# Dense products as pairs of 64-row halves with two outputs in two banks, in cycles of two attention steps

## The chip, the cores and the metric

The kernel runs on one core of a Trainium2 chip. The metric is device microseconds of one execution. Before the change the median of three runs is 1954.51 us (1954.01 to 1956.67).

## The reference

A layer norm of x (2048 x 512), and on it an attention block (32 heads of 16) and a gated MLP side by side; both are added to x.

```python
def _A_ref(x, wqkv, wo):                       # H = 32, Dh = 16
    qkv = (x @ wqkv).reshape(B, S, 3, H, Dh).transpose(2, 0, 3, 1, 4)
    q, k, v = qkv[0], qkv[1], qkv[2]
    p = softmax(einsum("bhqd,bhkd->bhqk", q, k) * Dh ** -0.5)
    o = einsum("bhqk,bhkd->bhqd", p, v)
    return o.transpose(0, 2, 1, 3).reshape(B, S, D) @ wo
def _B_ref(x, w_in, w_sp, b_sp, w_out):        # F = 1792, Fh = 896
    z = gelu(einsum("bsd,df->bsf", x, w_in))
    z2 = layernorm(z[..., Fh:])
    g = einsum("ts,bsf->btf", w_sp, z2) + b_sp[None, :, None]
    return einsum("bsf,fd->bsd", z[..., :Fh] * g, w_out)
xn = layernorm(x)
return x + _A_ref(xn, wqkv, wo) + _B_ref(xn, w_in, w_sp, b_sp, w_out)
```

## The kernel before, in words

Attention is cut into 1024 **steps**, one for each pair of heads (16), block of 512 queries (4) and block of 128 keys (16). A step has four pieces of work. `scores` (L978, tile `st`) makes the scores of two heads, 128 keys x 512 queries each: two TensorE matmuls that contract 50 rows, one on the upper and one on the lower half of the array. `exp` (L62, tile `pf`) is one ScalarE instruction over both (128 x 1024). `pv` (L952, tile `o`) multiplies the exponentials by V, in groups of four matmuls that each take 32 columns of the array; each such matmul of the program stands as two instructions in the trace (2560 in the program, 5120 in the trace). Ahead of the scores by LEAD = 27 steps runs a pass for the row maxima: `max_mm` (L656, tile `mx`), two matmuls that contract 48 rows, and `max_red` (L664), one VectorE reduction over 128 x 1024. After every 16 maxima five short VectorE instructions (`max_fin`, L677 to L683) and a round trip through DRAM put the maxima into the rows 48 and 49 of the query operand.

Everything else on TensorE is called **dense** here: q and k of the later heads (`qk`), the two halves of the MLP's first product (`z2p`, `z1p`), the spatial product (`sp`), the MLP's output (`mo`) and the attention's output (`ao`). `mm3` (L174 to L176) makes each product of fp32 operands from three matmuls over 128 rows (high x high, low x high, high x low), into one bank of PSUM. A dense tile is evicted by ScalarE or VectorE, and GpSimd does most of the elementwise work behind it.

The order of every engine is written by one loop over `half`. Two halves make a cycle of three steps. The first half issues scores, maximum, scores, the V products of earlier steps and the exponentials, the second half maximum, scores, maximum, and then as many dense products as a `credit` allows. The generators in `queue` yield the price of each dense product; `side` and `bg` hold the elementwise work that is let in a little per half; a clock of `HALF` us per half keeps account of GpSimd. Before step 0, 18 halves do maxima and dense products alone.

PSUM has eight banks: three tiles of two banks turn between scores and maxima (`spsum`), one bank takes dense products (`d`), one the V products (`o`).

Of the kernel before, what the change touches and what calls it, by code (L numbers as in the profile page):

```python
# [16 lines left out]
P = 128  # L17
S = 2048
D = 512
# [14 lines left out]
LEAD = 27  # L34
PF = 6
DENSE = 931
HALF = 2.7
# [3 lines left out]
def fused_block(ctx, tc, x, wqkv, wo, w_in, w_spT, b_sp, w_out, out):  # L41
# [14 lines left out]
    wide = []  # L56
# [43 lines left out]
    left = [0]  # L100

# [9 lines left out]
    now = [-2 * LEAD // 3 - 1]  # L111
# [18 lines left out]
    def later(k, fn, *args):  # L130
        late.append((now[0] + k, fn, args))
# [25 lines left out]
    def dpsum(nm, tag="d", n=1):  # L157
        left[0] = n
# [14 lines left out]
    def mm3(acc, lh, ll, rh, rl, first, last):  # L173
        nc.tensor.matmul(acc, lh, rh, start=first, stop=False)  # L174
        nc.tensor.matmul(acc, ll, rh, start=False, stop=False)  # L175
        nc.tensor.matmul(acc, lh, rl, start=False, stop=last)  # L176

# [26 lines left out]
    def prepare(out, loads, freed=None):  # L204
# [3 lines left out]
        while loads or flight or made:  # L208
# [8 lines left out]
            if loads and len(rawfree) > 0 and clock() >= rawfree[0] and (freed is None or freed and now[0] >= freed[0]):  # L217
# [4 lines left out]
                flight.append((now[0] + 2, k, begin(*a)))  # L222
# [51 lines left out]
    def turn_x(g, lo=0, hi=4):  # L274

        tiles = [spsum(f"xT{g}_{lo}_{c}") for c in range(3)]
        sl = slice(lo * P, hi * P)
        for c in range(ND):
            for i in range(lo, hi):
                nc.tensor.transpose(tiles[c % 3][:, c // 3, i * P:(i + 1) * P], xs[g, i][:, c * P:(c + 1) * P], ident)  # L280
        for c in range(ND):
# [3 lines left out]
            split(t[:, 0, sl], t[:, 1, sl], tiles[c % 3][:, c // 3, sl], (hi - lo) * P)  # L285
# [19 lines left out]
    def qk_group(m, g, w, tags=("d",)):  # L305
        for a in range(2):
            if now[0] < -2 and m:
                tags = ("d", "o")
            acc = dpsum(f"qk{m}_{a}_{g}", tags[a % len(tags)], ND)
            for c in range(ND):  # L310
                t = xnT[g, c]
                mm3(acc, w[a][:, 0, c * P:(c + 1) * P], w[a][:, 1, c * P:(c + 1) * P], t[:, 0, :], t[:, 1, :], c == 0, c == ND - 1)
                yield 650 + 0.5 * (c == ND - 1)
            if m == 0:
                run(qk_split(m, g, a, acc))
                yield 0
                continue
            raw_ = t512(f"qr{m}_{a}_{g}")
            act(raw_, acc, AF.Copy, 512)
            side.append(qk_split(m, g, a, raw_))  # L320
            yield 0
# [17 lines left out]
    def qk_rest():  # L339
        for g in range(NG):  # L340
            for m in range(1, 4):
                if m == 3 and g + 1 < NG:
                    fetch_xnT(g + 1, 1 if now[0] >= 0 else 0)
                while (m, 1) not in wq:
                    yield -1.5
# [4 lines left out]
                yield from qk_group(m, g, [wq[m, a] for a in range(2)])  # L350


    def v_tile(t, ws, mid=None):
        acc = dpsum(f"v{t}", "do"[t % 2])
# [15 lines left out]
    def gelu_out(x, u, n):  # L370

        gps(0.0011 * n).tensor_scalar(u, u, 1.0, 1.0, ALU.mult, ALU.add)
        gps(0.0024 * n).tensor_mul(x, x, u)

    def z2_norm(t, z):
# [7 lines left out]
        act(u, u, AF.Tanh, FH, scale=GC)  # L383
        late_ = t >= NT - 3
        if late_:
            act(u, u, AF.Identity, FH, bias=1.0)
        yield
        if late_:
            gps(0.0024 * FH).tensor_mul(z, z, u)
        else:  # L390
            gelu_out(z, u, FH)
# [18 lines left out]
        act(z, z, AF.Identity, FH, bias=rs[:, 2:3], scale=rs[:, 1:2])  # L410
        for j, (lo, w) in enumerate(((0, 512), (512, 384))):
            yield
# [4 lines left out]
            for a in range(2):  # L417
                store(z2scr[:, lo // P:(lo + w) // P, a, t, :], hl[:, a, :w].rearrange("p (f q) -> p f q", q=P), 1 + a)

    def z2_all():  # L420
        ws = w2
        wide.append(1)
# [8 lines left out]
        yield -3  # L431
        while len(ws) < 2 * ND:
            yield -1.5
        for t in range(NT):
# [3 lines left out]
            if t == NT - 2:  # L438
                wide.clear()
                prime()  # L440
                freed.append(now[0])
                bg.append(prepare(w1, [(f, f"w1_{f}", w_in[:, f * P:(f + 1) * P], D, ND) for f in range(NF)], freed))
            z = piece(f"z2_{t}").bitcast(F32).rearrange("p a b -> p (a b)")
            for j in range(2):
                acc = dpsum(f"z2p{t}_{j}", n=ND)
                for c in range(ND):
                    sl = slice(c * P, (c + 1) * P)
                    mm3(acc[:, :448], xt[:, 0, sl], xt[:, 1, sl], ws[c, j][:, 0, :448], ws[c, j][:, 1, :448], c == 0, c == ND - 1)
# [688 lines left out]
```

## Time and profile before

| what | value |
|---|---|
| median of the runs | 1954.51 us |
| span of the profiled execution | 1953.7 us, so 0.8 us below the median |
| TensorE busy | 1936.4 us (99%), 12559 matmuls |
| VectorE busy | 1373.9 us (70%) |
| ScalarE busy | 1233.1 us (63%) |
| GpSimd busy | 725.8 us (37%) |
| DMA | 284.23 MB, mean 145 GB/s |
| first maximum, first scores, last scores | 83.6, 138.1 and 1940.4 us |

Busy TensorE time is modelled from pipelined matmuls whose recorded durations overlap. The distance between two starts therefore says more than a duration does, and the view of the chain that ended last gives such distances directly.

### The profile page before, as it was taken

What the parts mean: (1) busy time and instruction counts of PE and PEld (TensorE: products, weight loads), DVE (VectorE), ACT (ScalarE), POOL (GpSimd) and SP (SyncE); (2) the same over time, 40 slices, a digit from 0 to 9 for tenths busy, and PEclk for the clock granted to TensorE, in tenths of its full rate; (3) what the DMA queues carried; (4) which work ended last, traced back from release to release, by engine and by line L of the source; (5) the groups of instructions that cost most, each with busy time, mean ns of one, the idle gap of its engine ahead of it and who ended that gap; (6) DMA issues with size and microseconds to landing.
All of it is one profiled execution on the core that took longest, in us unless ns stands there. A gap on an engine that the chain in (4) does not pass through costs nothing.

```text
span 1953.7 us, 32440 instructions
## 1 busy us (share of the span) xinstructions
PE 1936.4 (99%) x12559; PEld 1049.1 (54%) x12559; DVE 1373.9 (70%) x1567; ACT 1233.1 (63%) x1406; POOL 725.8 (37%) x789
## 2 busy tenths in 40 slices
PE   9999999999999999999999999999999999999998
PEld 7765555555555555555555555555555555555443
DVE  5357777777767677777777777777777777777872
ACT  5346778888777665656566656665566655555664
POOL 3334268889776931025122531017112400002100
PEclk9999999999999999999999999999999999999999
DMA  7566343463545635364545845346354735355323
GB/s 276 197 221 179 103 114 101 130 178 104 148 133 152 185 115 142 97 177 153 140 138 161 204 130 127 110 123 205 105 160 138 202 111 135 119 147 166 105 74 114
DMA packets 228466, 284.23 MB, mean 145 GB/s; under 512 B 34440, under 2 KB 133400, under 8 KB 225432
## 3 DMA queue, kind: packets, MB, share of 16 engines
q1 hardware_dynamic: 216360, 272.38, 48.3%
q0 software_dynamic: 2592, 8.46, 1.1%
q10 hardware_dynamic: 9360, 1.31, 0.4%
q8 instruction: 99, 1.62, 0.3%
q14 instruction: 55, 0.45, 0.1%
HBM read 188.51 MB, written 93.58 MB: 144 GB/s over the span
## 4 chain that ended last, share of the span: by engine, by line
PE 93%; DVE 2%; POOL 2%; DMA 1%; ACT 1%; issue 1%; SPq 0%; DVEq 0%; POOLq 0%; ACTq 0%
PE o L952 23%; PE mx L656 15%; PE st L978 15%; PE sp L174 7%; PE sp L176 5%; PE sp L175 5%; PE qk L174 2%; PE mo L174 2%; PE z1p L174 2%; PE qk L175 1%; PE qk L176 1%; PE z2p L174 1%; PE mo L175 1%; PE mo L176 1%; PE z1p L176 1%; PE z1p L175 1%
## 5 line engine op out<-in xcount | busy, mean ns | idle before, releaser
L664 DVE TENSOR_REDUCE mm<-mx 128x2 f32<-128x1024 f32 x1024 | 1222.1, 1222 | 498.6 <-PE mx L656 494.1
L62 ACT ACTIVATE pf<-st 128x1024 f32<-128x1024 f32 x1024 | 1028.6, 1025 | 621.7 <-PE st L978 589.1
L952 PE MATMUL o<-pf,vall 128*32 128x512 f32 (+1 forms) x5120 | 510.8, 513 | 0.0
L656 PE MATMUL mx<-kst,qst 48*128 48x512 f32 x2048 | 447.4, 434 | 2.5 <-ACT pf L62 1.6
L978 PE MATMUL st<-qst,kst 50*128 50x512 f32 x2048 | 443.2, 431 | 1.1 <-DVE mm L664 0.9
L656 PEld LDWEIGHTS mx<-kst,qst 48*128 48x128 f32 x2048 | 192.3, 185 | 268.3 <-ACT pf L62 175.6
L978 PEld LDWEIGHTS st<-qst,kst 50*128 50x128 f32 x2048 | 192.5, 185 | 159.6 <-issue 85.4
L952 PEld LDWEIGHTS o<-pf,vall 128*32 128x32 f32 x5120 | 131.5, 109 | 233.3 <-issue 211.1
L174 PE MATMUL sp<-wsp,zs 128*128 128x512 f32 x448 | 194.1, 433 | 0.3 <-DVE z1i L572 0.2
L579 POOL TENSOR_TENSOR z1i<-z1i,hhl 128x512 f32<-128x512 f32 x28 | 36.1, 1289 | 425.6 <-DVE z1i L572 395.1
L176 PE MATMUL sp<-wsp,zs 128*128 128x512 f32 x448 | 175.9, 393 | 0.0
L175 PE MATMUL sp<-wsp,zs 128*128 128x512 f32 x448 | 175.8, 392 | 0.0
L174 PEld LDWEIGHTS sp<-wsp,zs 128*128 128x128 f32 x448 | 83.8, 187 | 68.8 <-issue 51.7
L176 PEld LDWEIGHTS sp<-wsp,zs 128*128 128x128 f32 x448 | 84.1, 188 | 19.7
L175 PEld LDWEIGHTS sp<-wsp,zs 128*128 128x128 f32 x448 | 84.4, 188 | 12.1
L200 POOL CAST wo<-wo0r 128x512 fp32r<-128x512 f32 x1 | 0.6, 612 | 190.0 <-DMA wo0r<-in_wo 190.0
L329 POOL TENSOR_TENSOR qkhl<-qr,qkhl 128x512 fp32r<-128x512 f32 x24 | 31.0, 1290 | 75.0 <-ACT qkhl L62 75.0
L174 PE MATMUL z2p<-w,xt 128*128 128x448 f32 x128 | 51.3, 400 | 0.0
L174 PE MATMUL mo<-wout,hp 128*128 128x512 f32 x112 | 48.5, 433 | 0.6 <-DVE xr L616 0.4
L176 PE MATMUL z2p<-w,xt 128*128 128x448 f32 x128 | 46.9, 366 | 0.0
L175 PE MATMUL z2p<-w,xt 128*128 128x448 f32 x128 | 46.7, 365 | 0.0
L715 POOL TENSOR_TENSOR ob<-ob 128x512 f32<-128x512 f32 (+1 forms) x16 | 20.6, 1288 | 65.8 <-DMA ob<-rscr 59.1
(384 smaller groups left out, 1985.4 us busy)
## 6 DMA issues: line engine op xcount, KB each, us to landing
zs<-z2scr SPq DMA_DIRECT2D x112, 512.0 KB
escr<-e SPq DMA_DIRECT2D x60, 256.0 KB
hscr<-hhl SPq DMA_DIRECT2D x28, 512.0 KB
xscr<-xnT POOLq DMA_DIRECT2D x16, 512.0 KB, 4.8
qscr<-qkhl SPq DMA_DIRECT2D x16, 512.0 KB
kscr<-qkhl SPq DMA_DIRECT2D x16, 512.0 KB
xt<-xscr SPq DMA_DIRECT2D x64, 128.0 KB
z2scr<-z2hl SPq DMA_DIRECT2D x32, 256.0 KB
```

The lines of the kernel that those rows point to most:

```text
L62: return nc.scalar.activation(out, in_, func, **kw)
L174: nc.tensor.matmul(acc, lh, rh, start=first, stop=False)
L175: nc.tensor.matmul(acc, ll, rh, start=False, stop=False)
L176: nc.tensor.matmul(acc, lh, rl, start=False, stop=last)
L200: gps(0.6).tensor_copy(t[:, 0, :n], rw[:, :n])
L329: gps(1.3).tensor_sub(hl[:, 1 - a, :], src, hl[:, a, :].bitcast(F32))
L579: gps(1.3).tensor_add(z1, z1, hl[:, 1, :].bitcast(F32))
L656: nc.tensor.matmul(acc[:, j, :], qst[p % 2][rows, tt * P:(tt + 1) * P], kst[p % 2][rows, kc * 512:(kc + 1) * 512], start=True, stop=True)
L664: dve(1024).tensor_reduce(mmax[i // 16][:, :, t, kc], mstep.pop(i), AX.X, ALU.max)
L715: gps(1.3).tensor_mul(both[rows, 0, :], both[rows, 0, :], both[rows, 2, :])
L952: nc.tensor.matmul(acc[cols:cols + VW, a:a + w], vpack(kt - 1 + r, 2 * p + j), pf[:, j * 512 + a:j * 512 + a + w], start=(kt == 1 and a == ...
L978: nc.tensor.matmul(st[:, j, :], kst[p % 2][rows, kt * P:(kt + 1) * P], qst[p % 2][rows, c * 512:(c + 1) * 512], start=True, stop=True)
```

## The change

1. A dense product over 128 rows is cut into its upper and lower 64 rows (`lane`). Two outputs are made side by side in two banks (`d0`, `d1`): for two passes, `halves` runs output 0 on one half of the array and output 1 on the other, and then the other way round. An output without a partner (`whole`, the seventh column block of `z1p` and `sp`) has its halves in the two banks, and they are added at the eviction. One of the two outputs is evicted by VectorE, one by ScalarE.
2. A cycle is two steps, one per half. The first half issues a maximum, scores and all dense products, the second a maximum, scores and one round of V products (four matmuls of 512 columns for two steps).
3. PSUM: one tile of two banks for scores, three single banks for maxima, two for dense products, one for V products. `max_red` becomes two reductions over 128 x 512.
4. LEAD is 28 halves of one maximum each. The delays, the gating of `side` and `bg`, and the prices (now one per pair of matmuls) are restated in the new halves. The bias of the spatial product is added before the product with z1 and not after it. In the last group of `ao` 32 rows of zeros fill up 96 rows to 128. The tanh and the normalisation of `z2p` go in two instructions of half the width.

The core of the diff:

```diff
-LEAD = 27
+LEAD = 28
-HALF = 2.7
+HALF = 1.72
+SWAP, END = 1.25, 1.5
+    def spsum(nm):
+        return ps.tile([P, 2, 512], F32, tag="s", name=nm, bufs=1)
-    def spsum(nm):
+    def msum(nm):
         turns[0] += 1
-        return ps.tile([P, 2, 512], F32, tag=f"s{turns[0] % 3}", name=nm, bufs=1)
+        return ps.tile([P, 512], F32, tag=f"m{turns[0] % 3}", name=nm, bufs=1)
+    def lane(acc, half, prod, start, stop):
+        rows = slice(64 * half, 64 * half + 64)
+        nc.tensor.matmul(acc, prod[0][rows], prod[1][rows], start=start, stop=stop)
+    def halves(accs, parts, done=None):
+        flip = 0
...
+                    for j in range(3):
...
+                        for half in range(2):
+                            u = half ^ flip
+                            lane(accs[u], half, prods[u][j], first, last)
...
+                    yield END if last else SWAP if turn_ else 1
+                if step == 0:
+                    flip ^= 1
+    def evict(u, dst, src, n=512):
+        if u:
+            act(dst, src, AF.Copy, n)
+        else:
+            dve(n).tensor_copy(dst, src)
-        acc = mstep[i] = spsum(f"mx{i}")
+        accs = mstep[i] = [msum(f"mx{i}_{j}") for j in range(2)]
-        dve(1024).tensor_reduce(mmax[i // 16][:, :, t, kc], mstep.pop(i), AX.X, ALU.max)
+        for j, acc in enumerate(mstep.pop(i)):
+            dve(512).tensor_reduce(mmax[i // 16][:, j, t, kc:kc + 1], acc, AX.X, ALU.max)
-        for half in range(-2 * LEAD // 3, 2 * (N // 3 + 4)):
...
+        for half in range(-LEAD, N + 6):
...
+            max_mm(m)
+            if w == 0 and n is not None:
+                scores(n)
+            dense(half)
+            if w == 1 and n is not None:
+                scores(n)
...
+            if w == 1 and 0 <= b - 2 < N:
+                pv(b - 1)
+            if n is not None:
+                exp(n)
+            max_red(m)
```

What the recorded order has now is shown at three places. The first is TensorE in the stage of the spatial product (`sp`), one cycle long, from the last dense product of a cycle to the first of the next. Before, with `o` the V products and `sp` over 128 rows:

```order
L176 MATMUL sp_3_10231<-wsp_2_9062,zs_3_0_9983 128x512
L978 MATMUL st_10241<-qst_86,kst_88 128x512 x2
L656 MATMUL mx_10244<-kst_88,qst_86 128x512 x2
L978 MATMUL st_10247<-qst_86,kst_88 128x512 x2
L952 MATMUL o_1_10044<-pf_10175,vall 32x512 x2
L952 MATMUL o_1_10044<-pf_10199,vall 32x512 x2
L952 MATMUL o_1_10044<-pf_10209,vall 32x512 x2
L952 MATMUL o_1_10044<-pf_10224,vall 32x512 x2
L656 MATMUL mx_10264<-kst_88,qst_86 128x512 x2
L978 MATMUL st_10267<-qst_86,kst_88 128x512 x2
L656 MATMUL mx_10270<-kst_88,qst_86 128x512 x2
L174 MATMUL sp_3_10231<-wsp_3_9080,zs_3_0_9983 128x512
```

TensorE at the same stage of the change, where `sp_2_0` and `sp_2_1` are the two outputs and each row of them is one half of 64 rows:

```order
L189 MATMUL sp_2_1_13178<-wsp_12_12584,zs_3_3_13520 128x512
L189 MATMUL sp_2_0_13177<-wsp_12_12584,zs_2_3_13518 128x512
L799 MATMUL mx_0_13672<-kst_88,qst_86 128x512
L799 MATMUL mx_1_13673<-kst_88,qst_86 128x512
L1112 MATMUL st_13676<-qst_85,kst_87 128x512 x2
L1103 MATMUL o_2_13551<-pf_13627,vall 32x512 x2
L1103 MATMUL o_2_13551<-pf_13643,vall 32x512 x2
L799 MATMUL mx_0_13691<-kst_88,qst_86 128x512
L799 MATMUL mx_1_13692<-kst_88,qst_86 128x512
L1112 MATMUL st_13695<-qst_85,kst_87 128x512 x2
L189 MATMUL sp_2_1_13178<-wsp_12_12584,zs_3_3_13520 128x512
L189 MATMUL sp_2_0_13177<-wsp_12_12584,zs_2_3_13518 128x512
```

Between two groups of dense products there were three scores, three maxima and one visit of V products; now there are two maxima, two scores and one visit of four V matmuls.

The second place is VectorE in the same stage: before, one reduction a step.

```order
L664 TENSOR_REDUCE mm_13916<-mx_14117 128x2
L664 TENSOR_REDUCE mm_13916<-mx_14123 128x2
L664 TENSOR_REDUCE mm_13916<-mx_14147 128x2
L677 TENSOR_REDUCE mrow<-mm_13916 128x2x4
L678 TENSOR_REDUCE mn_14167<-mm_13916 128x8
```

VectorE in the change, around the eviction of one of the two `sp` outputs (`hhl`):

```order
L808 TENSOR_REDUCE mm_17052<-mx_0_17300 128x1
L808 TENSOR_REDUCE mm_17052<-mx_1_17301 128x1
L808 TENSOR_REDUCE mm_17052<-mx_0_17317 128x1
L808 TENSOR_REDUCE mm_17052<-mx_1_17318 128x1
L689 TENSOR_TENSOR hhl_6_17338<-sp_6_1_16986,hhl_6_17338 128x512
L808 TENSOR_REDUCE mm_17052<-mx_0_17349 128x1
```

Each reduction has become two, and the eviction stands between the reductions of two steps.

The third place is ScalarE there. Before, with `e` the eviction of a block of V products:

```order
L62 ACTIVATE pf_8594<-st_8585 128x1024
L62 ACTIVATE pf_8604<-st_8591 128x1024
L62 ACTIVATE e_3_8616<-o_3_8406 128x512
L62 ACTIVATE pf_8618<-st_8610 128x1024
L62 ACTIVATE pf_8640<-st_8631 128x1024
```

ScalarE in the change, with `hhl` the eviction of the other `sp` output:

```order
L63 ACTIVATE pf_17334<-st_17321 128x1024
L63 ACTIVATE hhl_6_17338<-sp_6_0_16985 128x512
L63 ACTIVATE pf_17360<-st_17353 128x1024
L63 ACTIVATE e_0_17364<-o_0_17015 128x512
L63 ACTIVATE pf_17391<-st_17374 128x1024
```

Over the whole of the change's order 321 of the 1023 places between two exponentials hold one other ScalarE instruction, one holds two, and the rest none; before, 163 held one and 54 held two to four.

More of the change, by code (lines that the diff above doesn't have):

```diff
@@ L110, in fused_block @@
     late = []
-    now = [-2 * LEAD // 3 - 1]
+    now = [-LEAD - 1]
     pool = [-1000.0]
@@ new lines, in whole @@
+    def whole(accs, part, done=None):
+        for i in range(len(part)):
+            while True:
+                prods = part[i]()
+                if prods is not None:
+                    break
+                yield -2
+            for j in range(3):
+                last = i == len(part) - 1 and j == 2
+                for half in range(2):
+                    lane(accs[half], half, prods[j], i == 0 and j == 0, last)
+                rem[0] = 3 * (len(part) - i) - j - 1
+                if j < 2:
+                    yield 1
+            if done:
+                done(0, i)
+            yield END if last else 1
@@ L274, in turn_x @@
     def turn_x(g, lo=0, hi=4):
-        tiles = [spsum(f"xT{g}_{lo}_{c}") for c in range(3)]
+        two = spsum(f"xT{g}_{lo}")
+        banks = [two[:, 0, :], two[:, 1, :]] + [msum(f"xT{g}_{lo}_{c}") for c in range(2)]
         sl = slice(lo * P, hi * P)
@@ L505, in z1_all @@
+                if end_ and f > 1:
+                    freed.extend([now[0] + 1] * len(fs))
                 yield 0
```

597 lines of the change are left out of this document (323 added, 274 removed).

## Prediction

> **What bounds the kernel now.** I read the page first, then the chain that ended last in the middle of the spatial product, then the instructions in order of time around one exponential, then the first and last uses of the score tile. From the page:
>
> ```profile
> span 1953.7 us, 32440 instructions
> ...
> PE 1936.4 (99%) x12559; PEld 1049.1 (54%) x12559; DVE 1373.9 (70%) x1567; ACT 1233.1 (63%) x1406; POOL 725.8 (37%) x789
> ...
> PE 93%; DVE 2%; POOL 2%; DMA 1%; ACT 1%; issue 1%; SPq 0%; DVEq 0%; POOLq 0%; ACTq 0%
> ...
> L664 DVE TENSOR_REDUCE mm<-mx 128x2 f32<-128x1024 f32 x1024 | 1222.1, 1222 | 498.6 <-PE mx L656 494.1
> L62 ACT ACTIVATE pf<-st 128x1024 f32<-128x1024 f32 x1024 | 1028.6, 1025 | 621.7 <-PE st L978 589.1
> ```
>
> TensorE carries 93% of the chain, and VectorE and ScalarE wait for TensorE: 494.1 us for maxima, 589.1 us for scores. So the kernel lasts as long as TensorE's own sequence. What a piece of it costs is in the chain, where each row runs until the next begins. One cycle of three steps, and one V visit of the next:
>
> ```profile
> 900.31 0.43 PE sp L174
> 900.74 0.23 PE sp L175
> ...
> 902.35 0.23 PE sp L176
> 902.58 0.43 PE st L978 x2
> 903.01 0.24 PE mx L656 x2
> 903.25 0.24 PE st L978 x2
> 903.49 1.43 PE o L952 x16
> 904.91 0.43 PE mx L656 x2
> 905.34 0.23 PE st L978
> 905.57 0.24 PE mx L656 x2
> 905.82 0.44 PE sp L174
> ...
> 909.02 1.85 PE o L952 x16
> ```
>
> Three prices stand here. A dense product over 128 rows takes 0.23 us, and so does a pair of 48- or 50-row matmuls on the two halves of the array. The first product after a change of shape (128 rows, two halves, four column strips) takes 0.43, so a change costs 0.20. A V visit: by the order both visits are of 16 trace instructions, the first half of 256 and half of 512 columns, the second all of 512; they differ by 0.42, which is one round of four at 512 (and two at 256). The visit that the change leaves, two trace rounds of 512, is therefore 1.43 - 0.42 = 1.01 us, its change of shape included. The cycle is 905.82 - 900.31 = 5.51 us, of which four changes of shape are about 0.7.
>
> For the mean of all cycles, and for both ends of the program:
>
> ```profile
> L656 PE MATMUL mx<-kst,qst x2048: 383/399/626, 83.6 to 1899.0; 48*128 48x512 f32 x187
> L978 PE MATMUL st<-qst,kst x2048: 386/396/794, 138.1 to 1940.4; 50*128 50x512 f32 x187
> ```
>
> From 138.1 to 1940.4 are 1802 us for 1023 steps, **1.76 us a step**, or 3.52 for two. Ahead stand 83.6 us of preparation and 54.5 us in which maxima run alone; behind the last scores are 1953.7 - 1940.4 = 13.3 us.
>
> **The change, part by part.** *Shapes.* If dense halves of 64 rows are of one shape with scores and maxima, both changes around a dense group go: 0.40 us a cycle, 341 times, 136 us. V visits rise from 341 to 512; each costs 1.01 - 2 x 0.42 = 0.17 and the 0.20 of the maximum behind it, so 171 x 0.37 = 63 us come back. The number of products stays: 2880 pairs of halves against 2880 whole ones, 0.23 each, by the rows of `mx` and `st` above. As a sum of TensorE alone, a cycle of two steps with D dense pairs is now: first half, score to score, (2 + D) x 0.23; second half, score 0.23, V visit 1.01, maximum 0.43, 1.67. (0.23 is 902.58 - 900.74 by eight products.)
>
> *One score tile.* This adds a wait that the trace of before does not have: with three tiles of two banks the next scores never waited for the last exponential. Now scores n+1 write where exponential n reads. Its links can be read off:
>
> ```profile
> 904.85 0.50 PE L656 MATMUL mx<-kst,qst 48*128 48x512 f32 x2
> 905.18 0.40 PE L978 MATMUL st<-qst,kst 50*128 50x512 f32 x2
> 905.42 0.40 PE L656 MATMUL mx<-kst,qst 48*128 48x512 f32 x2
> 905.68 1.03 ACT L62 ACTIVATE pf<-st 128x1024 f32<-128x1024 f32 x1 [0.51 <-PE st L978]
> ```
>
> ```profile
> 1940.98 1.02 ACT L62 ACTIVATE pf<-st 128x1024 f32<-128x1024 f32 x1 [2.12 <-PE st L978]
> 1942.05 0.20 PEld L952 LDWEIGHTS o<-pf,vall 128*32 128x32 f32 x6 [0.24 <-ACT pf L62]
> ```
>
> Scores at 905.18, exponential at 905.68: 0.50. The exponential: 1.02. Its end at 1942.00 releases a weight load at 1942.05: 0.05. And a matmul whose weights were not loaded ahead loses what the row at 904.85 loses against the next one, 0.33 against 0.24: 0.10 rounded. Score to score can't be less than 0.50 + 1.02 + 0.05 + 0.10 = **1.68 us** (the unrounded starts give 1.675). Behind the waiting scores stand the dense group, the V round and the next maximum, so this floor is TensorE's in each half. The second half (1.67) sits on it. The first half exceeds it from D = 6 on (8 x 0.23 = 1.84); with D = 5 it is 1.61 and waits. The 448-column products of `z2p` take less:
>
> ```profile
> 302.98 0.20 PE z2p L175
> ```
>
> Six of them and two pairs make 1.66, on the floor again.
>
> Counted over the whole order of the change, the 512 cycles have these D: 37 none, 29 one to four, 92 five, 286 six (61 of them `z2p`), 28 seven, 40 eight. First halves: 37 + 29 + 92 + 61 = 219 at 1.675 are 367 us, 225 at 1.84 are 414, 28 at 2.07 are 58, 40 at 2.30 are 92; second halves: 512 at 1.675 are 858. **Sum 1789 us**, 1.75 a step against 1.76 now. So the saved changes of shape are nearly all given back: 37 cycles without dense products and the floor take about 70 us of them, and the loop has more dense work than before, since fewer products run ahead of it (below).
>
> *Ahead of the loop.* Maxima alone: 28 halves, with 96 dense pairs by the order (216 whole products before, so 120 are moved into the loop, 28 us). TensorE needs (96 + 28) x 0.23 = 29 us. VectorE now reduces twice over 512. A reduction of 512 is not in the trace; the rows next to it are:
>
> ```profile
> 91.14 4.62 DVE L664 TENSOR_REDUCE mm<-mx 128x2 f32<-128x1024 f32 x4 [1.26 <-PE mx L656]
> 1947.89 1.89 DVE L839 TENSOR_TENSOR fin<-al,fin 128x512 f32<-128x512 f32 x3 [1.59 <-PE al L821]
> L776 DVE TENSOR_TENSOR fin<-ao,fin 128x512 f32<-128x512 f32 x16 | 10.9, 680 | 6.3 <-PE ao L176 6.3
> ```
>
> Three 512-wide operations end 1.89 us after the first starts, so one follows another after (1.89 - 0.68) / 2 = 0.60; four 1024-wide reductions follow each other by (4.62 - 1.23) / 3 = 1.13. Bounds for a pair are thus 1.13, if nothing is added, and 1.36, two whole durations of 0.68; I take 2 x 0.60 = 1.20, the closest row. Then 28 x 1.20 = 33.6, four evictions of 0.60 and one group of closing instructions of 0.8 make 37 us: VectorE sets this stage, and the first scores come at 83.6 + 37 = 120.4, 18 us sooner than now (15 to 22 us by the bounds).
>
> *VectorE in the loop.* 2 x 1.20 = 2.4 us in a cycle of 3.35 to 3.53, against 1.13 in 1.76. Three single banks let it lag by one reduction. The closing group fits:
>
> ```profile
> 112.02 0.19 DVE L677 TENSOR_REDUCE mrow<-mm 128x8 fp32r<-128x32 f32 x1
> ...
> 112.63 0.21 DVE L683 STREAM_TRANSPOSE ms<-mrow 128x32 f32<-128x32 f32 x1
> ```
>
> ```profile
> L397 DVE BATCH_NORM_STATS2 zst<-z 128x6 f32<-128x448 f32 x32 | 18.3, 613 | 0.0
> L398 DVE BATCH_NORM_AGGREGATE zmv<-zst 128x2 f32<-128x12 f32 x16 | 3.3, 209 | 0.6
> ```
>
> The closing group takes 0.82 us in 64 cycles, where 0.9 to 1.1 are free. Only the statistics of `z2p` (two at 0.61 and one at 0.21, 1.43) exceed that, by at most 0.5 in 16 cycles; between 0 and 8 us, I take 0.
>
> *ScalarE.* Between the end of an exponential and the next one's start lie 0.05 + 0.10 + 0.50 = 0.65 us. The one other instruction that the order has in 321 of these gaps is of 512 columns or less, 0.60 to 0.63:
>
> ```profile
> 1943.23 0.60 ACT L62 ACTIVATE e<-o 128x512 f32<-128x512 f32 x1 [1.23 <-PE o L952]
> ```
>
> It costs nothing if its input is there in time, and its own lateness if not. I take 0; the other end is a rival below. GpSimd's additions behind evictions and the DMAs keep their number (797 against 793 rows, 1089 on SP in both) and lie beside TensorE; GpSimd is busy for 37% of the span.
>
> *The end.* Four small products `nd` and five visits of `al` lie in the last halves and add about 6 us to the floor; behind the last scores the same 13.3 us follow.
>
> **Sum:** 120.4 + 1789 - 1.7 (the last half lies behind the last scores) + 6 + 13.3 = 1927, and with 4 us for evictions that wait for the last dense pair of their own half (76 groups at 0.05, the release above) 1931. The profiled execution lies 0.8 below the median, so **1932 us**, 1.2% less. Its own range: 1917, if the wait for weights (0.10) is hidden in the second halves and the first ones of D = 5, to 1955, with VectorE at its upper bound in the lead (5), the statistics (8), and 0.01 us on each half of the loop.
>
> **The rivals.** *TensorE's sum decides* (0.11). If exponentials let the score tile go sooner than their end, only products count: 512 x 1.67 + (1024 + 2400) x 0.23 + 384 x 0.20 = 1719, in all 1862. Against it speaks the release row at 1942.05; for it, that TensorE has waited for nothing so far.
>
> *The gaps on ScalarE* (0.19, slower). The other instruction of a gap starts late where it waits for dense products of its own half, for GpSimd or for a buffer, and each microsecond of that is then in the chain through the single score tile, as it was not with three. At 0.15 us on 321 places it costs 48 us: 1980. It decides from 0.08 us on, where the sum passes 1958. For it: the gap of 0.65 leaves 0.02 to 0.05 us. Against: first halves with D of 6 and more have 0.17 us besides, and the order keeps to one instruction in a gap.
>
> *A second matmul is not free* (0.04, slower). The trace shows at most three pairs in a row, and the change has runs of ten. The rows give 0.23 to 0.24 for a pair; if every dense pair takes 0.24, that is 0.01 x 2880 = 29 us: 1961, and a little less already decides. Against it speaks the difference of 0.42 above: 16 trace instructions in two rounds fit into it at 256 columns, 0.21 for eight loads and matmuls, more than a pair asks for. [...]
>
> *The change does not do what it says* (0.03). If 64-row halves count as another shape than 50-row ones, 475 dense groups keep their 0.40 us: 190 us more, 2122. Against: 48 and 50 rows follow each other at 0.23.
>
> **How the numbers follow.** Forecast 0.63: 0.54 of it lies below 1950.6, 0.06 within 0.2% of 1954.5 (what a measurement can tell from no change), 0.03 above. The first rival is faster (0.11), the other three slower (0.26), of the ScalarE rival 0.03 still within 0.2% and 0.03 below. So faster 0.68, same 0.09, slower 0.23. The range from 1885 to 1980 leaves out the first rival's core and the far ends of the slower ones, about 0.2.
>
> **What would show it.** The start of scores n to n+1 alternates between 1.84 and 1.68 us in `sp`; weight loads of `st` wait for ScalarE's `pf` as the longest of all waits; TensorE's dense pairs follow at 0.23 with no 0.43 around them; first scores near 120; VectorE's reductions 0.65 to 0.69 each. The forecast is wrong if dense pairs take more than 0.24, if scores in cycles without dense products come closer than 1.6 or farther than 1.75, or if ScalarE's other instructions end after the next scores are ready.

## The result and the profile after

The changed kernel takes **1972.3 us** (median of 4 runs, 1965.9 to 1975.9) against 1955.6 (4 runs, 1954.0 to 1957.3): ratio 1.0081, 95% interval 1.0062 to 1.0101. It is slower by 16.7 us (0.8%), where 1.2% faster was forecast; the forecast of 1932 is 40 us too low. The page of the changed kernel, in the parts that were shown of before:

```profile
span 1971.1 us, 37250 instructions
...
PE 1920.7 (97%) x14415; PEld 1078.4 (55%) x14415; DVE 1463.7 (74%) x2614; ACT 1268.2 (64%) x1430; POOL 730.6 (37%) x794
...
PE 89%; ACT 4%; DVE 4%; issue 1%; POOL 1%; DMA 1%; DVEq 0%; SPq 0%; ACTq 0%; POOLq 0%
...
L808 DVE TENSOR_REDUCE mm<-mx 128x1 f32<-128x512 f32 x2048 | 1307.2, 684 | 377.7 <-PE mx L799 372.9
L63 ACT ACTIVATE pf<-st 128x1024 f32<-128x1024 f32 x1024 | 1050.3, 1026 | 590.4 <-PE st L1112 574.9
...
L799 PEld LDWEIGHTS mx<-kst,qst 48*128 48x128 f32 x2048 | 218.6, 184 | 486.5 <-DVE mm L808 434.3
...
L1112 PEld LDWEIGHTS st<-qst,kst 50*128 50x128 f32 x2048 | 199.9, 185 | 117.0 <-ACT pf L63 75.6
```

TensorE is still the chain, with 89% of it where it had 93%. ScalarE and VectorE (4% each, 1% and 2% before) have taken the rest. The chain over one ordinary cycle of the changed kernel, in a dense product of the first MLP half:

```profile
661.71 0.43 PE mx L799 x2
662.13 0.26 PE st L1112 x2
662.39 1.39 PE z1p L189 x12
663.78 0.23 PE mx L799 x2
664.02 0.23 PE st L1112 x2
664.25 0.99 PE o L1103 x8
```

Six pairs take 1.39 us, 0.23 each, with no 0.43 at either edge: the halves share the shape of scores and maxima. A V round with its change of shape is 0.99, forecast 1.01. The prices hold in the whole loop too. Measured from the starts of all 1024 pairs of scores, sorted by the number D of dense pairs that the order puts between them:

| half | count | forecast | mean | median |
|---|---|---|---|---|
| first, D = 0 | 37 | 1.675 | 1.62 | 1.59 |
| first, D = 5 | 92 | 1.675 | 1.64 | 1.64 |
| first, D = 6 in `z2p` | 61 | 1.675 | 1.73 | 1.70 |
| first, D = 6 elsewhere | 225 | 1.84 | 1.88 | 1.86 |
| first, D = 7 | 28 | 2.07 | 2.09 | 2.09 |
| first, D = 8 | 40 | 2.30 | 2.44 | 2.31 |
| second | 511 | 1.675 | 1.73 | 1.68 |

The medians are right within 0.09 us. The means of the second halves and of D = 8 are not: a few halves are far longer. Both ends of the loop, from the views of the two tiles:

```profile
L799 PE MATMUL mx<-kst,qst x2048: 386/491/794, 83.4 to 1904.1; 48*128 48x512 f32 x187
```

```profile
L1112 PE MATMUL st<-qst,kst x2048: 386/404/793, 124.1 to 1954.9; 50*128 50x512 f32 x187
```

First scores came at 124.1 (forecast 120.4: +3.7); from there to the last scores are 1830.8 us (1797.3 with the allowances: +33.5); 16.2 follow (13.3: +2.9). These are the 40 us, and 33 of them lie in the loop.

**Where in the loop.** With the measured prices (the median of each row, and 1.62 for D = 0) the order sums to 1790 us, 3 more than the 1787 of the forecast for the same 1023 halves. 41 us stand above the prices, of which the forecast had allowed 10. 30 of the 41 stand in 32 halves. Four places hold 20.9: the first exponentials (124 to 134, 5.5), a single block of `z1p` (682 to 695, 4.4), and two in the spatial product (1028 to 1037, 4.4; 1430 to 1441, 6.6). Four visits of `al`, which the allowance foresaw, hold 3.1. The chain at the largest place of the changed kernel:

```profile
1425.35 5.07 DMA wsp_11r<-in_w_spT
...
1433.13 1.26 POOL wsp L279
1434.39 0.22 POOL os L853
...
1434.63 0.35 DVE os L855
1434.98 0.56 DVE mm L808
...
1435.58 0.79 PE mx L799
1436.37 0.43 PE st L1112 x2
1436.80 3.41 PE sp L189 x16
```

Read it downwards: a block of weights takes 5.07 us to land; GpSimd stands before it in its own order, then splits it and the next; behind them is a small addition of sums (`os`), whose reciprocal VectorE must do before its maxima; TensorE waits for a bank of the maxima. The other place in the spatial product has the same reciprocal in its chain, and the waits of the changed kernel have just these two:

```profile
DVE os L855 <- POOL os L853: 9.0, 2, 4.9
```

The kernel before has no such wait. Its GpSimd stands before blocks of these weights as long (23.2 us in all, 20.8 now), but each of its 16 reciprocals begins 3.4 us or more after the addition has ended. So at these two places the lateness itself came with the new order. The block of `z1p` is the seventh, the one without a partner, whose halves are added at the eviction:

```profile
681.52 0.59 ACT z L63
...
682.20 0.69 DVE z L607
682.89 0.61 DVE mm L808
...
683.54 0.49 PE mx L799
```

The addition waits for ScalarE's copy, and the maxima wait behind it. This alone costs 0.6 us. At the first exponentials an eviction of `qr`, its split and a row of 1.28 us without a tile (ACT_TABLE_LOAD) stand ahead on ScalarE.

At the largest place the rows after the wait are long: eight pairs in 3.41 us, 0.43 each. The windows of the changed kernel show why (the columns are the busy time of each engine; the last three are granted clock, DMA share and GB/s):

```profile
676.00:684.00 8.00, 7.83 (x60) 4.57 (x58) 5.95 (x10) 5.19 (x6) 5.39 (x7) 1.00 0.00 0
686.00:696.00 10.00, 9.96 (x40) 4.43 (x39) 4.91 (x12) 4.69 (x5) 4.77 (x5) 0.51 0.21 79
...
1430.00:1434.00 4.00, 1.77 (x13) 0.38 (x11) 0.00 (x0) 1.02 (x1) 3.30 (x4) 0.97 0.99 320
1434.00:1440.00 6.00, 4.42 (x20) 3.51 (x22) 2.69 (x5) 1.02 (x1) 4.76 (x7) 0.50 0.62 204
```

At each of the four places TensorE's granted clock falls to half (0.50), for 3.4 to 10.2 us, 27 us in all. In the 3.4 us ahead of these stretches 4, 12, 11 and 5 matmuls began, where the median of the loop is 26. These stalls are thus paid twice: once as a wait and once in longer rows (0.43 a pair for 0.23 at 1436.80); in `z1p`, whose next cycles hold no dense products, the second part is nearly all. Of the kernel before, the trace has one such stretch in the loop, 3.4 us at 141.5.

### The profile page after: what moved, and what is told of

Its sections match the earlier page's. It is cut to its first block, busy times and chain, and to the rows that moved or that the text cites. A ratio compares the mean times of both kernels' runs of the same rounds, so it can differ in the third digit from the quotient of the medians.

```text
span 1971.1 us, 37250 instructions
## 1 busy us (share of the span) xinstructions
PE 1920.7 (97%) x14415; PEld 1078.4 (55%) x14415; DVE 1463.7 (74%) x2614; ACT 1268.2 (64%) x1430; POOL 730.6 (37%) x794
## 4 chain that ended last, share of the span: by engine, by line
PE 89%; ACT 4%; DVE 4%; issue 1%; POOL 1%; DMA 1%; DVEq 0%; SPq 0%; ACTq 0%; POOLq 0%
PE o L1103 24%; PE mx L799 16%; PE sp L189 15%; PE st L1112 13%; PE z1p L189 4%; PE mo L189 4%; PE z2p L189 4%; ACT pf L63 3%; PE qk L189 3%; PE ao L189 2%; DVE mm L808 2%; PE v L176 1%; PE v L175 1%; PE v L177 1%; PE al L976 0%
## 5 line engine op out<-in xcount | busy, mean ns | idle before, releaser
L808 DVE TENSOR_REDUCE mm<-mx 128x1 f32<-128x512 f32 x2048 | 1307.2, 684 | 377.7 <-PE mx L799 372.9
L63 ACT ACTIVATE pf<-st 128x1024 f32<-128x1024 f32 x1024 | 1050.3, 1026 | 590.4 <-PE st L1112 574.9
L1103 PE MATMUL o<-pf,vall 128*32 128x512 f32 x4096 | 548.7, 608 | 0.0
L799 PE MATMUL mx<-kst,qst 48*128 48x512 f32 x2048 | 511.2, 450 | 20.5 <-DVE mm L808 17.9
L799 PEld LDWEIGHTS mx<-kst,qst 48*128 48x128 f32 x2048 | 218.6, 184 | 486.5 <-DVE mm L808 434.3
L1112 PE MATMUL st<-qst,kst 50*128 50x512 f32 x2048 | 448.6, 418 | 16.6 <-ACT pf L63 13.3
L189 PE MATMUL sp<-wsp,zs 64*128 64x512 f32 x2688 | 350.6, 391 | 0.0
L189 PEld LDWEIGHTS sp<-wsp,zs 64*128 64x128 f32 x2688 | 259.6, 186 | 46.4
L1112 PEld LDWEIGHTS st<-qst,kst 50*128 50x128 f32 x2048 | 199.9, 185 | 117.0 <-ACT pf L63 75.6
L1103 PEld LDWEIGHTS o<-pf,vall 128*32 128x32 f32 x4096 | 81.0, 108 | 166.1 <-issue 166.1
L189 PE MATMUL z2p<-w,xt 64*128 64x448 f32 x768 | 91.1, 363 | 0.0
L189 PE MATMUL mo<-wout,hp 64*128 64x512 f32 x672 | 87.0, 389 | 0.0
L189 PEld LDWEIGHTS z2p<-w,xt 64*128 64x128 f32 x768 | 75.1, 185 | 5.9
L189 PEld LDWEIGHTS mo<-wout,hp 64*128 64x128 f32 x672 | 64.4, 185 | 11.4
L757 POOL TENSOR_TENSOR xr<-mox,xr 128x512 f32<-128x512 f32 x8 | 10.2, 1275 | 151.1 <-ACT mox L63 119.4
L935 POOL TENSOR_TENSOR fin<-aox,fin 128x512 f32<-128x512 f32 x8 | 10.2, 1274 | 96.4 <-ACT aox L63 77.9
```

Of the source, the lines that this page charges most:

```text
L63: return nc.scalar.activation(out, in_, func, **kw)
L189: nc.tensor.matmul(acc, prod[0][rows], prod[1][rows], start=start, stop=stop)
L799: nc.tensor.matmul(accs[j], qst[p % 2][rows, tt * P:(tt + 1) * P], kst[p % 2][rows, kc * 512:(kc + 1) * 512], start=True, stop=True)
L808: dve(512).tensor_reduce(mmax[i // 16][:, j, t, kc:kc + 1], acc, AX.X, ALU.max)
L1103: nc.tensor.matmul(acc[cols:cols + VW, :], vpack(kt - 1 + r, 2 * p + j), pf[:, j * 512:(j + 1) * 512], start=kt == 1, stop=kt == NT - 1)
L1112: nc.tensor.matmul(st[:, j, :], kst[p % 2][rows, kt * P:(kt + 1) * P], qst[p % 2][rows, c * 512:(c + 1) * 512], start=True, stop=True)
```

## The experiments

Two theories stood at first. *Floor*: the single score tile (scores, exponential, scores) costs more than I charged. *Stalls*: the ordinary half costs what I said, and single late arrivals are now each in the chain, with no second score tile to absorb them. "Level" below is the changed kernel, 1972.3.

**Half an exponential.**

```
-act(pf, sts.pop(n).rearrange("p j q -> p (j q)"), AF.Exp, 1024, scale=0.25)
+act(pf[:, :512], sts.pop(n)[:, 0, :], AF.Exp, 1024, scale=0.25)
-nc.tensor.matmul(..., pf[:, j * 512:(j + 1) * 512], start=kt == 1, ...)
+nc.tensor.matmul(..., pf[:, :512], start=kt == 1, ...)
```

The 1024 is the length that the order is planned with; it stays, so that the order does not move. This kernel leaves out half of the exponentials.

> The change, but the exponential of a step covers only the first head's 512 columns, and both heads' V products read that half (the second head's probabilities are left out). Theory 1, the single score tile sets a floor of 1.68 us from scores to scores: the exponential falls from 1.03 to about 0.60 us and the floor to 1.25, so halves with D of 5 or less and all second halves go down to TensorE's own sum: 60 to 70 us less than the change, 1900 to 1912 us, and scores follow at 1.61 in first halves with D = 5. Rival, the floor is hidden anyway and what the change lost lies in longer dense pairs or in single stalls: within 10 us of 1972.

Measured: 1940.7 (1937.6 to 1947.8), ratio to before 0.993 (0.991 to 0.995). Between the two: 32 us below level. Halves with D = 0 fell from 1.62 to 1.24 us (1.25 expected), but D = 5 stayed at 1.63 and second halves at a median of 1.67: there TensorE's own sum is as long as the floor. So the floor is real and was priced rightly, but it binds in fewer halves than I thought: 24 of the 34 us that the loop lost lie in first halves with four pairs or fewer, 8 in second halves. The stalls of the spatial product stayed (1006, 1408).

**The sum of `os` on VectorE.**

```
-gps(0.3).tensor_add(sums[rows, 0, :], sums[rows, 0, :], sums[rows, 1, :])
-yield from pool_done()
+dve(32).tensor_add(sums[rows, 0, :], sums[rows, 0, :], sums[rows, 1, :])
```

> The change, but the two partial row sums of the output's normalisation are added on VectorE and not on GpSimd, so that VectorE's reciprocal waits for no GpSimd work. Theory 1, the stalls near 1028 and 1430 us are VectorE waiting for this sum, which stands on GpSimd behind the splitting of the spatial weights: they go, and with them the windows of half TensorE clock near 1034 and 1434, 9 to 14 us less than the change, 1958 to 1963 us. Rival, the late DMA of the weights or VectorE's load is the cause: the stalls stay or move to the next wait, 1968 to 1976 us.

Measured: 1997.0 (1990.3 to 2005.9): 25 us worse than level, which neither theory had. The planner keeps GpSimd's account by the clock, and the order of other work moved with it. The chain of this kernel in `z1p`:

```profile
579.13 1.28 DVE mm L808 x2
...
581.07 1.61 DVE z L559
582.68 0.61 DVE mm L808
...
583.34 0.50 PE mx L799
...
585.98 1.86 PE o L1102 x8
```

A multiplication of `z` that GpSimd used to do now meets VectorE's closing group of maxima; the next maxima are 2 us late in a run of empty cycles, and the V round behind them takes 1.86 instead of 0.99. The clock was half for 24 us from there, and for 32 us at the end. The new stall costs most (12 us up to 619). In the spatial product the rival was half right: the two waits for the addition are gone, but stalls of 5.2 and 4.6 us stand at 1035 and 1450, the second one TensorE's own wait for a transfer of `zs` that takes 7.76 us.

**Whole rows again.** Dense products over 128 rows again: the first pass makes output 0, the second output 1. The number of places and all else is as changed.

```
-for half in range(2):
-    u = half ^ flip
-    lane(accs[u], half, prods[u][j], first, last)
+nc.tensor.matmul(accs[step], *prods[step][j], ...)
```

> The change, but every dense product is again one matmul over 128 rows; the number of 0.23 us places and their order stay, the first pass makes output 0 and the second output 1. Theory 1, two changes of shape come back to each dense group, 0.40 us, less what the floor of 1.68 hides in first halves with D of 5 or less: 293 x 0.40 + 92 x 0.33 + 61 x 0.38 + a few = 170 us more than the change, 2130 to 2150 us. Rival, long runs of half products cost more than 0.23 each, so that the halves gain less: below 2100 us.

Measured: 2135.1 (2132.0 to 2140.9), as expected. Halves with D = 5, 6, 7, 8 went to medians of 2.05, 2.28, 2.50 and 2.75: 0.41 to 0.44 a group, two changes of shape. They sum to 177 us, and the lead took 10 more; the second halves got back 26 (mean 1.682 for 1.733): with 0.4 us of slack in a cycle most stalls vanish. Only 12 halves, with 10.6 us, stand more than 0.3 us above their medians, and the clock is half for 3.4 us of the loop, although VectorE still idles 1.4 and 1.9 us before the same two reciprocals. The part of the change that removes shapes gives 163 us on this schedule.

**Two score tiles of one bank.** Head 0's scores are paired with head 1's maximum, two exponentials of 512.

```
-return ps.tile([P, 2, 512], F32, tag="s", name=nm, bufs=1)
+return [ps.tile([P, 512], F32, tag=f"s{j}", name=f"{nm}_{j}", bufs=1) for j in range(2)]
...
+    scores(n, [0])
+    max_mm(m, [1])
+    dense(half)
...
+        scores(n, [1])
+        max_mm(m, [0])
```

> The change, but the two heads of a step go their own ways: two single banks for scores, two exponentials of 512 columns, and head 0's scores are paired with head 1's maximum ahead of the dense or V products of a half, head 1's scores with head 0's maximum behind them. Number and price of TensorE's pairs stay. Theory 1: each bank has 0.50 + 0.60 + 0.15 = 1.25 us of chain in a half of 1.6 or more, so the floor is gone, at about 0.1 us more of ScalarE time a step: 60 to 90 us less than the change, 1885 to 1912 us. Rival, TensorE is held by something other than the score tile: 1950 or more.

Measured: 1997.6 (1995.7 to 2000.1): the rival. In `sp` a cycle with D = 5 did fall, from 3.36 to 3.29 us (median, from V round to V round), but one with D = 6 stayed at 3.53, and the stages with much elementwise work grew. Chain and waits of this kernel:

```profile
403.56 0.59 ACT pf L63
404.14 0.70 ACT z L63
404.85 0.49 ACT pf L63
...
405.38 0.49 PE st L1115
```

```profile
PEld st L1115 <- ACT pf L63: 434.0, 653, 3.1
```

An instruction of ScalarE between the two exponentials now delays the second bank by 0.70 us; waits of score weights for exponentials rose from 75.6 to 434.0 us. A second small tile bought nothing here, where ScalarE's order puts other work between.

**The reciprocal four halves later.**

```
 yield from pool_done()
+for _ in range(4):
+    yield
 dve(256).reciprocal(sums[rows, 1, :], sums[rows, 0, :])
```

> The reciprocal of the sums of a chunk of heads (VectorE) is written four halves later, behind GpSimd's addition of these sums. Theory: the two long stalls of the changed kernel (1028 to 1038 us and 1429 to 1440 us, together 11 us above the prices of their halves) come from this reciprocal, which stands ahead of the maxima on VectorE and waits for an addition that GpSimd reaches late, behind the weights of the spatial product. With it four halves (about 7 us) later both stalls and the half-clock windows behind them should go: 1957 to 1964 us. Rival: GpSimd's lateness shows in the next thing that waits for it, and the time stays within 5 us of 1972.

Measured: 1970.8 (1965.4 to 1974.8): no change in sum, but not for the rival's reason alone. The stalls at 1028 and 1430 and the half clock behind them are gone, and the spatial product, from its first row to its last, fell by 10.0 us. New ones stand at 596 to 609 and 633 to 641 (11 us). The chain of this kernel there:

```profile
591.65 7.90 DMA oscr<-ohl
...
599.66 0.52 ACT z2hl L63
600.18 0.92 ACT pf L63
...
601.15 0.80 PE st L1114 x2
```

The chunk's last step, now later, holds one of three buffers that `z2hl` needs; ScalarE waits for the store, with the exponential behind it.

**The dense work ends later.**

```
-pace = 2 * todo / max(N - 18 - half, 8)
+pace = 2 * todo / max(N - 4 - half, 8)
```

> One number: the dense work is spread so as to end 4 steps before the last scores instead of 18. Theory of the floor: the halves of the last 25 us stand at 1.68 us with three pairs or fewer, and would take five at no cost, so work moved there makes cycles elsewhere shorter. By the prices of a half (1.62 without pairs, 1.64 with five, 1.85 with six, 2.09 with seven, 2.31 with eight) the loop's sum falls from 1798 to 1793: 1964 to 1969 us. Rival: the last additions now come behind the last exponentials and lengthen the end by as much: 1972 or more.

Measured: 1976.4 (1968.5 to 1983.8), inconclusive. The median lies on the rival's side, but the rival's longer end is not seen (15.1 us, 16.2 at level). In the profiled run, the fastest of the four, the loop is 5 us shorter, as the prices say; the runs spread over 15 us, the slower the lower their mean clock (0.992 to 0.983).

**Queries and keys in the pauses of `z1p`, with the later reciprocal.** `qk_pair(3, g, ...)` is called where `z1_all` waits for its blocks.

> The queries and keys of the last 128 columns are computed in the pauses of the first dense product (z1) instead of ahead of it, so that twelve of the 37 cycles without pairs are filled with work; with the later reciprocal of the run beside it. By the prices of a half the loop's sum falls from 1798 to 1792, and the two stalls should give 11 us: 1952 to 1958 us, about the kernel before. Rival: GpSimd, which sets the pauses of z1, has ten microseconds more to do there, new stalls take the place of the empty cycles, and the time stays above 1960.

Measured: 1982.4 (1977.7 to 1983.5): the rival. D = 0 fell from 37 halves to 25, but the mean of the second halves rose to 1.76, and the clock was half at six places of the loop (41 us).

**Filling pairs in empty cycles.**

```
+if half >= 0 and not k and between and not drain:
+    accs = dpair(f"fill{half}")
+    for i in range(4):
+        for j in range(2):
+            nc.tensor.matmul(accs[j], qst[0][rows, 0:P], kst[0][rows, 0:512], ...)
```

> In each of the 37 cycles without dense pairs four pairs of products are added whose results nobody reads. A half with four pairs costs no more than an empty one (1.60 against 1.62 us), so the pairs themselves are free. Theory: TensorE's granted clock falls to half where a stall meets cycles in which TensorE has little to do; with the pairs the half-clock stretch from 686 to 696 us shrinks to 3.4 us or goes, and the time is 1960 to 1970 us. Rival one: the clock doesn't depend on it, the stretches stay, 1970 to 1975 us. Rival two: the empty half's room isn't there, and each pair costs its 0.23 us: 34 us more, above 2000 us.

Measured: 1969.3 (1967.2 to 1972.4), at the upper edge of the theory. The same window as above, of this kernel:

```profile
686.00:696.00 10.00, 9.95 (x77) 5.02 (x76) 7.97 (x18) 7.49 (x10) 5.91 (x7) 1.00 0.22 81
```

In the same 10 us 77 matmuls ran where 40 had: the clock stayed full, and `z1p` fell by 4 us. D = 0 stayed at 1.62: the pairs are free. The stalls of the spatial product stayed, and some half clock with them (3.4 us each, 3.4 and 6.8 at level), though the cycles there are full of dense products. So the pairs removed the half clock that came in thin cycles behind a lateness of 0.6 us, worth 4 us, and not the half clock behind the stalls of the spatial product.

**Three places at once:** filling pairs, the later reciprocal from half 390 on, the first evictions of `qr` on ScalarE (`evict(a if now[0] > 2 else 1, ...)`).

> Three places at once: the pairs without use in empty cycles (as in the run with filling pairs); the reciprocal four halves later, but only from the spatial product on (where that took 10 us off, while earlier in the program it made new stalls); and the first two evictions of queries and keys on ScalarE, so that the first exponentials don't wait behind VectorE's maxima. Theory: what the changed kernel lost against the forecast lies in single stalls at places, which add up: 1972 less 3 to 4 (fill), less 10 (reciprocal), less 3 to 5 (start): 1953 to 1957 us. Rival: the lateness of VectorE and GpSimd is passed on and shows up in the next wait wherever one is removed: 1962 us or more.

Measured: 1961.4 (1958.3 to 1962.7), ratio to before 1.0031 (1.0019 to 1.0042): 11 us below level, the lowest median of a kernel that does the whole work, but short of the 1953 to 1957 that the theory gave and just under the rival's 1962. The loop is 14.2 us shorter (1816.6); the end is 3.2 longer, with filling pairs behind the last scores. Halves more than 0.3 us above their price hold 14.4 us instead of 30.0. So most of what the three cures gave adds up here.

**Two V rounds every four steps.**

```
-if w == 1 and 0 <= b - 2 < N:
-    pv(b - 1)
+if w == 1 and b % 4 == 0:
+    for q in (b - 3, b - 1):
...
```

> V products of two rounds in every fourth half instead of one round in every second: the part of the change that the forecast charged with 63 us is undone, and nothing else. If TensorE's sum decided, 256 changes of shape to V and back would go, 0.37 us each: 95 us less, about 1877 us. Theory of the floor: dense pairs stand only in first halves, so a second half without V products (0.46 us of TensorE) stays at the floor of 1.68, while the one with both rounds takes 0.23 + 1.85 + 0.43 = 2.51 instead of 1.68: 0.83 us on each of 256, about 2180 us.

Measured: 2214.6 (2210.4 to 2217.2): the floor's side, and beyond. The chain of this kernel:

```profile
1000.61 0.24 PE st L1112 x2
1000.84 1.85 PE o L1103 x16
1002.70 0.43 PE mx L799 x2
1003.12 0.24 PE st L1112 x2
...
1005.14 1.03 ACT pf L63
...
1006.22 0.50 PE st L1112 x2
```

The V half has the expected 2.51 us (1003.12 less 1000.61; median 2.54), and the second half without V waits for its exponential, at a median of 1.60. The clock was half for 147 us of the loop, which the expectation did not count; that is a likely reason, not a shown one, for the 35 us beyond it. Fewer changes of shape, and 242 us more: the price saved in halves that sit on the floor was worth nothing here.

**The three places and the later end together.**

> The three places of the run beside it and the dense work spread so as to end 4 steps before the last scores instead of 18. By the prices of a half the loop's sum falls by another 5 us (it did in the profile of that edit alone, while the times of its runs went up): 1948 to 1953 us, just ahead of the kernel before. Rival: denser cycles in the spatial product leave ScalarE and GpSimd later, and the edit costs as it did in the runs alone: 1957 us or more.

Measured: 1968.5 (1964.6 to 1971.4): the rival. Three new stalls (halves that are 7.0 us too long at 1419, 3.5 at 1797, 2.5 at 1938) and the long rows behind them ate what three cures had given; the first begins, like the one shown above, with a block of `wsp` that takes 6.00 us to land.

**Weights split later.**

```
-flight.append((now[0] + 3, k, begin(*a)))
+flight.append((now[0] + 5, k, begin(*a)))
```

> The changed kernel with one number altered: GpSimd splits a block of weights five halves after its transfer was issued, not three (8.7 us instead of 5.2). Theory: the stalls around 1030 and 1430 us begin with GpSimd standing before a block that has not landed (transfers of 5 to 6 us), and the addition and the reciprocal behind it, with the maxima, wait in the same line. With the block landed first these stalls go without touching addition or reciprocal: 1959 to 1966 us. Rival: the lateness comes from the addition's own data or from GpSimd's load, and the time stays at 1968 to 1976.

Measured: 1962.0 (1957.8 to 1973.1, 10 runs), ratio to before 1.0046 (1.0029 to 1.0064). The place at 1028 is gone, the one at 1430 down from 6.6 to 2.2 us and begins with another transfer (7.43 us, `zs`), as the theory had it. That the total fits is in part luck: the start and the block of `z1p` lost 5.5 and 4 us too, unforeseen, and a new stall of 6.6 came at 580. Nor did GpSimd's waits for blocks shrink: they are 25.0 us in all, against 20.8 at level; they no longer stand ahead of the additions. The chain of this kernel at the new stall:

```profile
578.88 2.35 DVE mm L808 x4
581.23 1.07 DVE zst L480 x2
...
582.55 0.26 ACTq L1215
...
583.49 0.92 ACT pf L63
```

VectorE's statistics of `z2` stand among maxima, and ScalarE, which issues the transfer of the last chunk's maxima, waits for VectorE with the exponential behind it.

**Places and weights together.**

> The kernel of the three places with the later splitting of weights, and with the filling pairs left out behind the last scores, where they cost 3.4 us in its chain. Theory: 1961 less 3.4, less 0 to 4 for small stalls: 1954 to 1958 us, level with the kernel before, since what remains above the forecast are the prices of a half (9 us) and the visits of the last products. Rival: the later weights delay dense work into new waits: 1961 us or more.

Measured: 1965.8 (1963.8 to 1970.5): the rival. The end did shrink to 16.2 us behind the last scores, but three stalls eat more. The one at 584 (5.1) is the one shown above, from the later weights; at 480 (5.1) a filling pair itself waits for a transfer of the queries that it reads, and at 1534 (6.2) TensorE waits for a transfer of `zs`, 11.36 us long. No version that does the whole work beat the kernel before.

## Why the prediction was wrong

- **Shapes: right.** Pairs at 0.23, no 0.43 around dense groups, 0.41 to 0.44 a group when undone.
- **The rival of the second matmul: fell.** 12 matmuls in 1.39 us, 0.23 a pair in runs of six.
- **The floor: right within 5%** (medians of 1.59 to 1.70 for a forecast of 1.675; halves with D = 0 are the 1.59, just under the 1.6 that I gave as a sign of being wrong, with a mean of 1.62). TensorE's sum as the only bound (1862) fell with it; two V rounds at a time showed it most.
- **The order's D and the sum: right within 3 us** of 1787 on the same halves. Second halves and those with D = 6 cost 11 us more, those with five pairs or fewer 8 less.
- **The lead: 3.7 short.** VectorE's reductions followed each other at 0.60 to 0.61, as taken (0.684 each, overlapping). But VectorE idled for 3.7 us: 0.5 to 0.6 behind each eviction of `qr`, until TensorE had made the next maximum, and the rest in gaps of 0.1.
- **The forecast's own range, 1917 to 1955.** The lower end goes beyond its condition: by the halves that it names it would be 1923. The measured time lies 17 us above the upper end.
- **The failed step** is the one that took the other engines' work in the loop at nothing: VectorE's extras, of which it named only the statistics, and ScalarE's ("I take 0" for both), and "GpSimd's additions behind evictions and the DMAs", which "lie beside TensorE". That holds nearly in 990 halves, where 11 us stand above the prices. In some 30 halves something arrives late, behind a transfer of 5 us or a meeting of two long instructions, and 30 us stand there, 3 of them the forecast visits of `al`. The runs show this from several sides: the chains at the places, the cures (three places at once take 14 us off the loop), and whole rows, where with slack in each cycle most stalls vanish.
- **Why these arrivals are late, and why they count,** is shown in part only. At the two places in the spatial product the lateness is new: the kernel before has its reciprocals 3.4 us or more behind the additions. The addition at the eviction of `z1p` is new too. That the three score tiles of before would have let TensorE run on is argued: no run gives a bank back. Nearly every shift of the order drew new stalls, and in some of them TensorE waits for its own operands, which more score tiles would not help.
- **The rival "gaps on ScalarE" (1980)** came nearest in time, and is half right. Its 321 small latenesses fell: from scores to exponential are 0.513 us (median) with another instruction in the gap and 0.516 without. Its condition, an instruction that waits "for GpSimd or for a buffer", is what happened, at a handful of places and on VectorE more than on ScalarE. That its time comes so near is luck.
- **The sign that did not come:** the longest wait of weight loads should have been `st` for `pf`; it is 75.6 us against 434.3 for `mx` on VectorE. The matmuls themselves idle for only 13.3 and 17.9 us behind the same two by the whole trace, so such waits of loads are mostly not on the path, and the floor hides in longer rows: 0.50 for a pair of scores that waited, 0.24 for one that did not.
- **The change does what it says;** the rival at 2122 fell.
- **Clock:** I took TensorE's clock as full. It was half for 27 us of the loop; the longer rows are part of the stalls' 30 us.

What stays open: why runs of one kernel spread by 10 us and more (1965.9 to 1975.9 here, 1957.8 to 1973.1 with later weights, 3 us before). Their times follow the mean clock (0.994 to 0.989 here), so stalls probably come or go between runs of one order; only one run of each kernel has a trace, so this was not seen. Differences of 10 us between two kernels rest on such medians, and the places on one trace each. Open is also where the 11 us in the other 990 halves come from.

## What to carry to other kernels

When buffers are taken from the pipeline that paces the kernel, sum the ordinary cycle, and then price the late arrivals apart: list what stands ahead of the pacing instruction in the order of each engine (a split that waits for a transfer, a reciprocal, a store's buffer), and ask how late it can be and how many buffers absorb that. Compare the distances with the old order: a reciprocal that stood 3.4 us or more behind its addition came to stand right behind it. A saving of changes of shape counted here only in cycles whose sum is above the floor (two V rounds at a time saved 256 changes to V and back and took 242 us more). Where an order has no reserve, try a cure at one place on the whole kernel, since it can move other work into the same trap.

## What the runs showed of the hardware

- TensorE's granted clock fell to half (0.50) within a kernel whose TensorE is 97% busy: in the 4 us from 1430 to 1434, where such a stretch begins, it was busy for 1.77 of 4.00. In the loop of the changed kernel the stretches last 3.4, 6.8 or 10.2 us. What sets the clock is not shown. Ahead of the stretch at 686 TensorE was busy for 2.92 of 3.40 us by the profile, but only 12 matmuls began there; with four unread pairs in each empty cycle the clock stayed full from 686 to 696 (1.00 for 0.51).
- Two exponentials of 512 columns from PSUM in each of 1024 steps kept ScalarE busy for 1146.7 us (596 ns each, overlapping; two score tiles) against 1050.3 for one of 1024; reductions of 512 follow each other at 0.61 us, two to a step, against 1.13 for one of 1024 in the kernel before. Splitting a PSUM tile in two cost 0.09 us a step on either engine.
